# w_in in three loads, shifted V in halves, and a moved order table: an attention and gated feed-forward kernel on one core

## The chip, the cores and the metric

One core of one Trainium2 chip. The metric is the device time of one execution in microseconds (us), median over several runs. Lower is better. Each run is marked fast or slow: slow when it is more than 1.5% above the fastest run of the same kernel. Ratios are of fast runs; a median given below takes in every run. In the profile of before PE runs the matmuls (2,720), DVE, ACT and POOL the elementwise work (467, 474 and 203 operations), and SP issues all but a few transfers.

## The reference

Eight batches of 576 positions, eight heads of 64. Attention inside a window of 32 positions to either side, then a feed-forward block: a product with w_in (512 x 1024), a rectifier, a convolution over three positions in each feature, a sigmoid gate, a product with w_out (1024 x 512).

```python
mask = np.abs(pos[:, None] - pos[None, :]) <= 32
attn = softmax(np.where(mask, scale * q @ k.T, -1e9))
x = (attn @ v)                       # to (8, 576, 512)
h = np.maximum(x @ w_in, 0.0)
conv_out[:, s] = sum(conv_w[k] * hp[:, s + k] for k in range(3))   # hp: h with a zero row at each end
out = (h / (1.0 + np.exp(-conv_out))) @ w_out
```

## The kernel before

The program is a list of some 1,550 operations. A string, the order table, says in which order they are issued, on which engine (P is PE, V is DVE, S is ACT, G is POOL, D is a transfer on SP's queue, Q one on ACT's), and which buffers they take. Each engine works through its part strictly in that order.

```python
BUFS = {'st': 3, 'qkb': 5, 'qkT': 3, 'attn': 2, 'rec': 4, 'xn': 3, 'hT0': 8, 'hT1': 6, 'hT2': 6, 'cp': 2, 'gT': 4, 'y': 7}
ORDER = """
15D 11D0 12D 1F 17D 2F 13D1 2F 14D 7F 28G 0V 1P0 ...      # number, engine, buffers; "7F": seven filler matmuls
"""
    for number, engine, buffers in re.findall(r"(\d+)([A-Z])(\d*)", order):
        ...
        o.emit(engine)
```

V is needed in two alignments: `ve` as cast, and `vo` shifted by 64 positions across the partitions, which in batches 2 to 7 is a transfer:

```python
    def shift_v(b, c0, c1):
        op(f"vo hi {b} {c0} {c1}", lambda e: copy(e, vo[0:64, c0:c1], ve[64:128, c0:c1]), ...)
        op(f"vo lo {b} {c0} {c1}", lambda e: copy(e, vo[64:128, c0:c1], ve[0:64, c0 + 1:c1 + 1]), ...)
    ...
        for c in range(NBLK - 1) if b < 2 else (0,):
            shift_v(b, c, c + 1 if b < 2 else NBLK - 1)
```

The convolution of a unit (128 features of a chunk of 384 positions, 12 chunks of 8 units) can be done in six ways: each tap is a matmul with a diagonal matrix on PE, a multiplication on POOL, or a fused multiply and add on DVE.

```python
    #        PE taps      POOL taps  DVE taps
    TAPS = {
        "3": ((0, 1, 2), (), ()), "2": ((0, 2), (), (1,)), "1": ((0,), (), (1, 2)),
        "q": ((), (0, 2), (1,)), "r": ((), (0,), (1, 2)), "s": ((0,), (1, 2), ()),
    }
    CONV = ('33333333', '33q3323r23223321', ..., '2rrr2rrq')      # one letter for each unit
```

The softmax here doesn't subtract the row's maximum and nothing guards it: scores larger than these inputs give would overflow.

## Time and profile before

| | before |
|---|---|
| median of runs | 228.67 us |
| span of the profiled run | 225.6 us |
| PE, DVE, ACT, POOL busy | 211.5, 197.3, 187.5, 137.7 us |
| first input matmul, last matmul | 25.80, 221.71 us |

In a line of the timeline the columns are start, duration, engine, source line, operation, output and inputs, shapes, count and, in brackets, the idle time of the engine before it and what ended that. A line of the waits has the total, the number and the longest of a kind of wait. In the table by stage each engine has its busy us and its number of instructions. The prediction shows the lines of before.

One view that the prediction did not ask for is the table for the whole stretch from the first input matmul on:

```profile
26.00:226.00 200.00, 190.17 (x2391) 108.25 (x2389) 179.62 (x412) 168.79 (x429) 117.85 (x139) 1.00 0.80 202
```

From 25.80 us to PE's last matmul at 221.71 are 195.9 us, and PE is shown busy for 190.4 of them (190.17 in this view, and 0.2 before 26 us). That leaves 5.5 us in which it does nothing, a number that matters below.

### The profile page before, as it was taken

The page shows a single profiled execution, that of the slowest core. Times are in us where ns is not written, and L with a number is a line of the kernel's source. Part 1 is how long each engine was busy: PE and PEld are TensorE (multiplying, and loading weights), DVE is VectorE, ACT ScalarE, POOL GpSimd, SP SyncE. Part 2 cuts the span into 40 slices and gives each one's busy share as a digit, 9 for nine tenths or more (in the row PEclk, how much of TensorE's full clock was granted, in tenths as well). Part 3 has the DMA queues.
Part 4 walks back from the last instruction along what each step waited for, and adds up shares of the span by engine and source line. Part 5 has one row for each costly group of instructions (what it writes and reads, how often), then busy time and mean ns, then how long its engine had stood idle before and what let it go on. Part 6 is the DMA issues. An engine that isn't in the chain of part 4 may idle for free.

```text
span 225.6 us, 7189 instructions
## 1 busy us (share of the span) xinstructions
PE 211.5 (94%) x2720; PEld 122.9 (54%) x2720; DVE 197.3 (87%) x467; ACT 187.5 (83%) x474; POOL 137.7 (61%) x203
## 2 busy tenths in 40 slices
PE   7698899989989999989999998999999999999993
PEld 5366567658555655545555454545655565455541
DVE  6279869899999979797999788989999999899990
ACT  2689899998989889879889989689989999777642
POOL 5978654654376937695368736756386735566640
PEclk9889999999999999999999999999999999999999
DMA  6999999999989999999997989994535212501224
GB/s 201 331 285 358 355 266 281 321 308 253 290 170 324 317 175 287 236 306 224 288 347 129 202 278 358 182 231 147 144 36 118 99 46 49 175 1 49 93 101 178
DMA packets 66391, 48.16 MB, mean 214 GB/s; under 512 B 50781, under 2 KB 50805, under 8 KB 66357
## 3 DMA queue, kind: packets, MB, share of 16 engines
q1 hardware_dynamic: 64992, 46.32, 78.6%
q10 hardware_dynamic: 1364, 1.39, 2.9%
q8 instruction: 21, 0.34, 0.8%
q14 instruction: 14, 0.11, 0.2%
HBM read 32.52 MB, written 9.44 MB: 186 GB/s over the span
## 4 chain that ended last, share of the span: by engine, by line
PE 41%; DVE 18%; ACT 17%; DMA 13%; issue 5%; SPq 3%; POOL 2%; DVEq 0%; ACTq 0%; POOLq 0%
PE pf L232 41%; DMA st<-in_k_dram 7%; ACT attn L232 6%; DVE pf L232 5%; DVE gT L232 4%; SPq L232 3%; DMA out_dram<-y 3%; ACT xn L232 3%; DVE qkT L232 2%; ACT pf L232 2%; DMA vo<-ve 2%; DVE attn L232 2%; DVE xn L232 2%; ACT qkb L232 2%; ACT y L232 1%
## 5 line engine op out<-in xcount | busy, mean ns | idle before, releaser
L232 PE MATMUL pf<-xT,w_in_sb 128*128 128x385 bf16 (+2 forms) x416 | 73.4, 315 | 3.6 <-ACT hT L232 0.9
L232 PE MATMUL pf<-w_out_sb,gT 128*128 128x512 bf16 x288 | 72.2, 380 | 0.0
L232 POOL TENSOR_SCALAR cp<-hT,conv_w_sb 128x384 f32<-128x384 bf16 (+1 forms) x63 | 38.9, 622 | 46.1 <-ACT hT L232 20.2
L232 ACT ACTIVATE pf<-pf 128x384 f32<-128x384 f32 (+1 forms) x104 | 48.2, 477 | 13.1 <-DVE pf L232 11.1
L232 DVE SCALAR_TENSOR_TENSOR gT<-pf,hT 128x384 bf16<-128x384 f32 (+1 forms) x104 | 52.1, 517 | 5.5 <-ACT pf L232 5.1
L232 PEld LDWEIGHTS <-w_in_sb 128*128 128x128 bf16 x416 | 38.6, 98 | 27.8 <-issue 4.5
L232 ACT ACTIVATE attn<-pf 128x512 bf16<-128x512 f32 (+1 forms) x96 | 41.4, 522 | 1.8 <-PE pf L232 1.8
L232 ACT ACTIVATE hT<-pf 128x385 bf16<-128x385 f32 (+2 forms) x76 | 35.4, 487 | 6.0 <-PE pf L232 5.6
L232 PEld LDWEIGHTS <-gT 128*128 128x128 bf16 x288 | 26.0, 98 | 25.7 <-DVE gT L232 0.5
L232 DVE SCALAR_TENSOR_TENSOR pf<-hT,conv_w_sb,pf 128x384 f32<-128x384 bf16 (+1 forms) x61 | 34.7, 586 | 1.2 <-PE pf L232 1.1
L232 PE MATMUL pf<-hT,diag_w 128*128 128x384 bf16 (+1 forms) x153 | 30.9, 309 | 0.9 <-DVE xn L232 0.6
L232 POOL TENSOR_SCALAR qkb<-st 128x1152 bf16<-128x1152 f32 (+1 forms) x23 | 25.7, 1122 | 7.6 <-DMA st<-in_k_dram 3.2
L232 DVE COPY qkT<-pf 128x576 bf16<-128x576 bf16 x35 | 25.6, 750 | 4.9 <-PE pf L232 4.9
L232 POOL TENSOR_TENSOR cp<-cp,cp 128x384 f32<-128x384 f32 (+1 forms) x24 | 24.4, 1016 | 1.6
L232 DVE TENSOR_TENSOR attn<-attn,mask 128x1152 bf16<-128x1152 bf16 x26 | 23.0, 886 | 2.4 <-ACT attn L232 2.3
L232 ACT ACTIVATE xn<-pf,rec 128x64 bf16<-128x64 f32 x96 | 22.0, 360 | 1.5 <-DVE rec L232 1.5
L232 ACT COPY y<-pf 128x512 f32<-128x512 f32 x30 | 18.1, 605 | 3.9 <-PE pf L232 3.7
L232 DVE SCALAR_TENSOR_TENSOR pf<-hT,conv_w_sb,cp 128x384 f32<-128x384 bf16 (+1 forms) x35 | 21.2, 618 | 0.0
L232 POOL TENSOR_TENSOR attn<-attn,mask 128x1152 bf16<-128x1152 bf16 x6 | 14.2, 2371 | 8.4 <-ACT attn L232 8.4
L232 DVE TENSOR_TENSOR xn<-pf,rec 128x256 bf16<-128x256 f32 x48 | 18.9, 410 | 0.0
L232 ACT COPY qkT<-pf 128x576 bf16<-128x576 bf16 x29 | 18.6, 664 | 0.4 <-PE pf L232 0.2
L232 PEld LDWEIGHTS <-diag_w 128*128 128x128 bf16 x153 | 13.3, 97 | 9.8 <-issue 1.3
(49 smaller groups left out, 235.2 us busy)
## 6 DMA issues: line engine op xcount, KB each, us to landing
st<-in_q_dram SPq DMA_DIRECT2D x16, 576.0 KB, 6.8
out_dram<-y SPq DMA_DIRECT2D x36, 256.0 KB, 3.8
st<-in_k_dram SPq DMA_DIRECT2D x14, 576.0 KB, 8.2
vst<-in_v_dram SPq DMA_DIRECT2D x24, 256.0 KB, 7.0
vst<-in_v_dram SPq DMA_DIRECT2D x15, 192.0 KB, 5.7
vo<-ve SPq DMA_DIRECT2D x11, 260.0 KB, 5.6
st<-in_moe_w_in_dram SPq DMA_DIRECT2D x2, 1024.0 KB, 9.3
st<-in_moe_w_out_dram SPq DMA_DIRECT2D x2, 1024.0 KB, 9.4
```

Source lines behind the costliest of these rows:

```text
L232: return lambda *args, **kwargs: fixed(do(*args, **kwargs))
```

## The change

The intent: start the w_in casts after half a megabyte, let attention start on the first half of the shifted V, and shift convolution work from DVE to PE, with an order table made anew for it. The core of the diff (the order table itself is replaced nearly everywhere and cut here):

```diff
-BUFS = {'st': 3, 'qkb': 5, 'qkT': 3, 'attn': 2, 'rec': 4, 'xn': 3, 'hT0': 8, 'hT1': 6, 'hT2': 6, 'cp': 2, 'gT': 4, 'y': 7}
-TURNS = ('eeeee', 'eeede', 'eeeed', 'dedde', 'ddddd', 'ddddd', 'ddddd', 'edddd')
+BUFS = {'st': 3, 'qkb': 6, 'qkT': 4, 'attn': 2, 'rec': 9, 'xn': 2, 'hT0': 7, 'hT1': 8, 'hT2': 9, 'cp': 3, 'gT': 3, 'y': 5}
+TURNS = ('eeeee', 'eeede', 'eeeed', 'dddde', 'ddddd', 'ddddd', 'ddddd', 'deddd')
 CONV = (
     '33333333',
-    '33q3323r23223321',
-    's222r32q',
-    '1232s332',
-    '22q22q22',
+    '33q3323r23q23321',
+    's222r32s',
+    '12323332',
+    '22q22s22',
     'q31s2qrq',
-    '33212q2s',
-    'r2rq312q',
-    'qq23q1q2',
-    'r3rqrq23',
-    '12qrrq1q',
-    '2rrr2rrq',
+    '33222q2s',
+    '13rq312s',
+    'qq33q1q3',
+    'r2rqqq23',
+    '233rrs2q',
+    '3s112qrr',
 )
 ...
+    gpsimd.memset(outside, 0.0)           # and four affine_selects on it: for another form
+    ...                                   # of the mask, which no unit uses here
 ...
+    W_PARTS = {"in": ((0, 2), (2, 4), (4, MB)), "out": ((0, MB // 2), (MB // 2, MB))}
 ...
-        for c in range(NBLK - 1) if b < 2 else (0,):
-            shift_v(b, c, c + 1 if b < 2 else NBLK - 1)
+        for c in range(0, NBLK - 1, 1 if b < 2 else 2):
+            shift_v(b, c, c + (1 if b < 2 else 2))
```

## The prediction

> **What bounds the kernel now.** I read the page's busy shares and slices first, then the table by stage, then the start and the end of the timeline, and the waits last.
>
> ```profile
> PE 211.5 (94%) x2720; PEld 122.9 (54%) x2720; DVE 197.3 (87%) x467; ACT 187.5 (83%) x474; POOL 137.7 (61%) x203
> ...
> PEclk9889999999999999999999999999999999999999
> DMA  6999999999989999999997989994535212501224
> ```
>
> PE leads with 94%, but the matmul ends are modelled and 75 filler matmuls are in it, so it must be checked against DVE's 87%. The DMA engines are nearly full until slice 26 (about 146 us) and then empty out. The table by stage (window and its length, busy us of PE, PE's weight loads, DVE, ACT and POOL with instruction counts, then PE clock, DMA share, GB/s):
>
> ```profile
> 0.00:26.00 26.00, 21.33 (x331) 14.66 (x332) 17.63 (x57) 18.73 (x46) 19.87 (x65) 0.93 0.98 299
> 26.00:40.00 14.00, 13.87 (x191) 9.26 (x190) 10.97 (x22) 12.84 (x31) 7.31 (x11) 1.00 1.15 290
> 40.00:80.00 40.00, 38.48 (x618) 24.40 (x616) 39.28 (x103) 36.19 (x99) 24.72 (x28) 1.00 1.06 282
> 80.00:140.00 60.00, 56.60 (x794) 31.61 (x792) 52.01 (x124) 54.07 (x138) 38.22 (x41) 1.00 1.08 258
> 140.00:200.00 60.00, 59.50 (x685) 32.49 (x684) 57.98 (x128) 51.90 (x133) 36.66 (x46) 1.00 0.52 120
> 200.00:220.00 20.00, 20.00 (x103) 9.90 (x102) 19.38 (x38) 12.14 (x27) 10.94 (x15) 1.00 0.19 69
> ```
>
> From 40 us on, PE and DVE are both close to full, in turn: DVE is the fuller one at 40 to 80 us, PE elsewhere. Only the first 26 us have room, and there PE runs fillers. The start and end of PE's timeline:
>
> ```profile
> 25.80 2.13 PE L232 MATMUL pf<-xT,w_in_sb 128*128 128x385 bf16 x12 [0.29 <-DVE xT L232]
> ...
> 29.99 0.70 PE L232 MATMUL pf<-ident,qkb 64*128 64x64 bf16 x36
> 30.62 0.83 PE L232 MATMUL pf<-xT,w_in_sb 128*128 128x385 bf16 x4
> ```
> ```profile
> 209.94 1.48 PE L232 MATMUL pf<-xT,w_in_sb 128*128 128x385 bf16 x8
> ...
> 214.28 7.43 PE L232 MATMUL pf<-w_out_sb,gT 128*128 128x512 bf16 x33
> ```
>
> The first feed-forward matmul starts at 25.80 us and waits for xT, not for w_in. Back-to-back rates follow: 33 output matmuls in 7.43 us less one 0.38 latency, 0.220 us each; eight 385-column ones in 1.48 less 0.33, 0.165 each; 36 transposes in 0.63 (to the next start), 0.0175 each; scores, 18 in 0.39 elsewhere in the trace, 0.022; attention times V, pairs 0.031 apart, 0.016 each. With the counts of the groups, PE needs 288x0.220 = 63.4, input matmuls 352x0.165 + 64x0.083 = 63.4, diagonal (convolution) matmuls 118x0.165 + 35x0.083 = 22.4, attention and turns about 35: 184 us without fillers. An eighth of the attention (4.4) lies before 25.8, so PE has 179.8 us to do in the 195.7 us from 25.8 to its last matmul at about 221.5: 92%. DVE has 197.3 - 17.6 = 179.6 there: also 92%. ACT has 168.8. So from 25.8 us on the kernel is bound by PE and DVE together, with about 16 us of slack in pieces; startup is 25.8 us and the end about 4 us.
>
> The waits (total us, times, longest):
>
> ```profile
> DVE rec L232 <- PE pf L232: 2.7, 5, 1.7
> ...
> PE pf L232 <- DMA xT<-xn: 0.5, 1, 0.5
> ...
> POOL w_in_sb L232 <- DMA st<-in_moe_w_in_dram: 0.5, 1, 0.5
> ...
> PE pf L232 <- DMA vo<-ve: 0.3, 1, 0.3
> ```
>
> The two transfers that the change divides cost 0.3 us (shifted V, plus up to 2 us in the reciprocals behind it) and 0.5 us (w_in, on POOL).
>
> [...]
>
> **The change part by part.** I decoded the order table by the program's own numbering and counted operations per engine.
>
> *w_in in three loads.* Two transfers of 1 MB become 512 KB, 512 KB and 1 MB; same bytes. POOL's first cast starts at 18.53 when the first MB has landed. At about 340 GB/s (rate of slices 4 and 5) half a MB less is 1.5 us sooner. POOL also has other work there, and the first input matmul waits for xT. On the path: 0 to 0.5 us.
>
> *Shifted V in halves.* Before, 11 transfers of 260 KB (5.6 us median to landing); after, 23 of 130 KB and a small one. Bytes are the same to 0.1 MB of 48. Twelve more issues at 0.54 us put 6.5 us on SP's queue, which has long waits to hide them. The first half may land 0.5 us sooner, the second no sooner. Worth 0 to 0.7 us in all.
>
> *Startup order.* On ACT two more evictions of q/k transposes (about 0.54 each) and one xT eviction (0.65); DVE loses two evictions (1.5), one V shift (0.3) and two xT copies (1.0). DVE is the path from 19.4 to 25.8, ACT before. DVE's last mask of batch 0 began at 20.81 because DVE was occupied, not because ACT was late, so about 1 us of DVE is gained and part is handed to ACT. Fillers fall from 75 to 50, 17 of these ahead of the first transpose[...]. Sum: -0.5 us, give or take 1.5.
>
> *Kinds of convolution units.* Diagonal matmuls: full width 118 to 138, half width 35 to 33: +20x0.165 - 2x0.083 = +3.1 us of PE; one turn goes from PE to DMA, -0.2. Of these, the last two chunks take 8 to 19, +1.8 us in the stage with PE at 20.00 of 20.00.
> DVE: taps 96 to 81 at 0.61 = -9.2; sums 4 to 8 at 0.56 = +2.2; relus +2 at 0.55; normalisations +2 at 0.41; masks +1 at 0.89; q/k evictions -3 at 0.75; xT -2; V casts +2 at 0.45; one y copy +0.7: together -6.4 us, of which some 2.6 in the startup.
> ACT: +3 evictions, +1 cast, -2 normalisations of four pieces (0.92 each), -2 relus and small ones: +0.4. POOL: about -5, and it has slack.
>
> So after the startup PE's need rises from 179.8 to 182.7 and DVE's falls from 179.6 to 175.8.
>
> *Buffers.* Fewer y (7 to 5), gT (4 to 3), xn (3 to 2); more qkT, qkb, hT1, hT2, cp, rec. Stores land in 3.8 us and outputs are 36 in 180 us, so five y suffice on average; a copy can still wait where stores queue behind SP's other work.
>
> **The sum.** Added PE work +2.9; startup -0.5; both transfers -0.7; PE and DVE no longer equally full. That last term is a choice: of the 16 us of slack I expect about 4.5 to go, because DVE, which PE and ACT wait for, is at 90% instead of 92% and the order was moved throughout with it. Sum: 2.9 - 0.5 - 0.7 - 4.5 = -2.8, so 228.7 becomes about 225.8.
>
> **The rivals.** (1) PE is the whole bound: the added 2.9 us appears in full and slack stays at 16. For it: PE 20.00 of 20.00 in the end stage and 59.50 of 60 before it. Then 230 to 231. (2) DVE was the real bound, PE only filled its latencies: the 3.8 us less on DVE after the startup and the startup gain appear, with less waiting besides. For it: 39.28 of 40 at 40 to 80 us, 57.98 of 60 later, and the diagonal matmuls being bought on purpose. Then 221 to 224. (3) Loading is the bound until 146 us: DMA shares over 1.0, and the bytes do not change. Against it: PE's direct waits for DMA are under 1 us. Then the time stays at 228 whatever the order. (4) Fewer buffers make new waits (ACT or DVE for y or gT behind a store): +1 to +3.
>
> **Range and chances.** Two percent under 228.67 is 224.1; that needs 4.6 us, rival 2 or a startup shorter by over 2 us. Two percent over is 233.2, which needs rivals 1 and 4 together. Range 221.5 to 229.5. Chances: faster 0.28, within 0.68, slower 0.04.
>
> **What would show it.** First input matmul at 25 to 26 us; diagonal matmuls 138 of full width; DVE about 191 us, PE's busy less by its fillers (some 4 us) and more by 3; PE's waits for vo gone; the last 33 or so output matmuls still back to back. Wrong if the first input matmul moves by over 2 us, if 40 to 140 us changes its PE fill by more than 4 us, or if waits for y or gT appear.

Cut from the text: under the startup order, the clause for a term of +0.3 us, a lower clock on the first transposes, which was the author's estimate and not shown by a trace. That term is still inside the startup's -0.5 us, and so inside the sum, which came to -2.8 us: 228.7 to about 225.8.

## The result, and the profile after

The changed kernel is correct and slower: 240.55 us (238.49 to 242.12, four runs, one of them slow) against 228.77 us. The ratio is 1.0494, 95% interval 1.0413 to 1.0575. A ratio here is the mean time of one kernel's fast runs over the mean of the other's of the same rounds, so it is not quite the ratio of the medians. The profiled run is a fast one.

The page of the changed kernel, busy shares and slices:

```profile
PE 215.2 (90%) x2709; PEld 122.7 (51%) x2709; DVE 197.0 (82%) x460; ACT 187.7 (78%) x468; POOL 135.5 (57%) x206
...
PEclk9999799999999999999999979999999999999999
```

PE's share fell from 94 to 90%, although it has more to do. The clock row has two dips, in slices 5 and 24. The table by stage:

```profile
40.00:80.00 40.00, 36.92 (x538) 23.38 (x535) 35.72 (x90) 35.52 (x98) 23.41 (x28) 1.00 0.96 263
80.00:140.00 60.00, 54.38 (x804) 30.54 (x805) 52.07 (x119) 51.69 (x124) 34.32 (x36) 1.00 0.96 232
...
28.00:240.00 212.00, 197.82 (x2407) 111.19 (x2405) 181.32 (x407) 167.48 (x420) 113.82 (x133) 0.98 0.73 192
```

Against before, PE's fill falls from 38.48 to 36.92 at 40 to 80 us and from 56.60 to 54.38 at 80 to 140. ACT falls with it, DVE falls at 40 to 80 us and stands at 52 at 80 to 140: no engine has become fuller there. DVE's busy time over the whole run is 197.0 us against 197.3, although it has 7 operations fewer; the prediction had about 191. The start of PE's timeline:

```profile
27.27 0.66 PE L234 MATMUL pf<-ident,qkb 64*128 64x64 bf16 x18 [1.17 <-POOL qkb L234]
...
28.06 3.96 PE L234 MATMUL pf<-xT,w_in_sb 128*128 128x385 bf16 x16
```

The first input matmul is at 28.06, not 25.80, and sixteen of them take 3.96 us where twelve took 2.13: this is half clock, shown as 0.50 from 27.05 to 30.46 us. PE waited 1.17 us for a cast on POOL just before it, and ACT's copy of the first block of xT, which stands ahead of it too, began at 26.71 us in place of 24.54. At the end 43 output matmuls run back to back from 225.83 us for 9.44 us, as the last 33 did before, so PE's last matmul ends at 235.27 us, 13.6 later. The account of these 13.6 us:

| term | before | after | difference |
|---|---|---|---|
| first input matmul | 25.80 | 28.06 | +2.3 |
| PE busy from there on | 190.4 | 197.8 | +7.4 |
| PE idle from there to its last matmul | 5.5 | 9.4 | +3.9 |

Of the +7.4 us busy, two spells of half clock (from 27.05 and from 139.69 us, each 3.41 us long at 0.50 in the trace, each thus worth 1.7 us of work) are 3.4, the added diagonal matmuls 2.9 by the prediction's count, and 1.1 I can't assign. The waits say where PE starved:

```profile
DVE rec L234 <- PE pf L234: 9.3, 8, 5.1
...
PE pf L234 <- DMA vo<-ve: 2.9, 2, 1.8
```

The waits for `vo`, which the prediction said would be gone, are now 2.9 us in place of 0.3. They lie in batch 5, as does DVE's longest wait of 5.1 us. Here is PE, then SP's queue:

```profile
139.72 0.26 PE L234 MATMUL pf<-vo,attn 128*64 128x65 bf16 x1 [1.79 <-DMA vo<-ve]
```
```profile
131.26 0.50 SPq L234 DMA_DIRECT2D vo<-ve  x1
131.85 1.25 SPq L234 DMA_TRANSPOSE xT<-xn  x1
133.15 0.58 SPq L234 DMA_DIRECT2D vst<-in_v_dram  x1
133.78 1.87 SPq L234 DMA_DIRECT2D vo<-ve  x3
```

The four halves of batch 5 are issued between 131.26 and 135.65 us, with a transposing transfer and a load between them, though the casts they copy from were done at 118 us. In SP's single queue they stand behind transposing transfers (the four issued from 128.03 to 137.05 us hold it for 1.25 to 1.35 us each) and behind loads of V.

A last view is my own: each PE operation that both traces have, matched by name, and by how much it starts later than before (median over the stretch, in us, by the time in the kernel before). I call it the ladder. An operation that was moved back in the order counts as late too, so a single column is exact only where the order is the same.

| kernel | 10-20 | 20-30 | 30-40 | 60-70 | 80-90 | 120-130 | 130-140 | 160-170 | 220-end |
|---|---|---|---|---|---|---|---|---|---|
| changed | +0.4 | +1.8 | +4.5 | +6.1 | +7.6 | +7.6 | +11.7 | +12.0 | +13.1 |

The loss comes in steps, and little of it is given back.

### The profile page after: what moved, and what is told of

Its sections match the earlier page's. It is cut to its first block, busy times and chain, and to the rows that moved or that the text cites. A ratio compares the mean times of both kernels' runs of the same rounds, so it can differ in the third digit from the quotient of the medians.

```text
span 239.3 us, 7142 instructions
## 1 busy us (share of the span) xinstructions
PE 215.2 (90%) x2709; PEld 122.7 (51%) x2709; DVE 197.0 (82%) x460; ACT 187.7 (78%) x468; POOL 135.5 (57%) x206
## 3 DMA queue, kind: packets, MB, share of 16 engines
HBM read 32.52 MB, written 9.44 MB: 175 GB/s over the span
## 4 chain that ended last, share of the span: by engine, by line
PE 55%; DMA 16%; DVE 11%; ACT 7%; SPq 6%; issue 3%; POOL 0%; ACTq 0%; DVEq 0%
PE pf L234 55%; DMA st<-in_q_dram 10%; SPq L234 6%; DMA st<-in_k_dram 4%; DVE gT L234 3%; DVE pf L234 2%; ACT pf L234 2%; DVE qkT L234 2%; DMA vo<-ve 2%; ACT qkb L234 1%; ACT attn L234 1%; DVE attn L234 1%; DVE hT L234 1%; ACT xn L234 1%; DVE vo L234 1%
## 5 line engine op out<-in xcount | busy, mean ns | idle before, releaser
L234 PE MATMUL pf<-xT,w_in_sb 128*128 128x385 bf16 (+2 forms) x416 | 75.7, 321 | 1.4 <-ACT attn L234 0.6
L234 ACT ACTIVATE pf<-pf 128x384 f32<-128x384 f32 (+1 forms) x104 | 46.6, 468 | 13.2 <-DVE pf L234 8.3
L234 PE MATMUL pf<-hT,diag_w 128*128 128x384 bf16 (+1 forms) x171 | 36.0, 313 | 3.3 <-ACT hT L234 1.9
L234 DVE SCALAR_TENSOR_TENSOR pf<-hT,conv_w_sb,pf 128x384 f32<-128x384 bf16 (+1 forms) x54 | 31.4, 588 | 1.1 <-PE pf L234 0.6
L234 DVE COPY qkT<-pf 128x576 bf16<-128x576 bf16 x32 | 23.5, 748 | 5.9 <-PE pf L234 5.8
L234 ACT COPY qkT<-pf 128x576 bf16<-128x576 bf16 x32 | 20.5, 653 | 4.4 <-PE pf L234 4.3
L234 DVE TENSOR_TENSOR attn<-attn,mask 128x1152 bf16<-128x1152 bf16 x27 | 21.1, 783 | 2.8 <-ACT attn L234 2.8
L234 PEld LDWEIGHTS <-diag_w 128*128 128x128 bf16 x171 | 15.4, 97 | 14.6 <-issue 3.7
L234 DVE SCALAR_TENSOR_TENSOR pf<-hT,conv_w_sb,cp 128x384 f32<-128x384 bf16 (+1 forms) x27 | 18.8, 707 | 0.7 <-issue 0.3
L234 PEld LDWEIGHTS <-attn 128*64 128x64 bf16 x576 | 12.4, 112 | 13.5 <-issue 8.9
```

What stands on the lines that cost most here:

```text
L234: return lambda *args, **kwargs: fixed(do(*args, **kwargs))
```

## The experiments

Eighteen kernels ran. "Changed" is the changed kernel, "before" the kernel before. Times are medians of four runs if nothing else is said. Runs of one group shared a chip (the last two runs of the fourth had one of their own), and ratios are to runs of before on that chip (median 227.5 to 228.8 us in every group; one execution of before in the second group took 403.48 us, counts as slow and is in no ratio). A half-clock spell comes in some runs of a kernel and not in others (the four runs of a_vo5 have mean clocks of 1.000, 0.989, 0.990 and 0.991), so a difference of less than about 2 us between two medians is not read as an effect; the ladders of profiled runs, where one sees which spells there were, are used for that.

### First group: what starts the lateness

The changed order puts a small shifted-V transfer of batch 0 on SP's queue ahead of the w_in loads. It might hold them up. Three runs place that one shift elsewhere. A fourth moves batch 5's halves.

**a_shift_dve**: changed, that shift back on DVE.

```diff
-37D
+37V
```

> The changed kernel with one V shift (batch 0, block 2, upper half) moved from SP's DMA queue back to DVE; nothing else. Queue theory: on SP's in-order queue this shift waited for the cast on ACT until 12.32 us and held back the w_in loads (12.90 instead of 8.70) and the batch 1 loads; undone, w_in is issued near 8.7, the first input matmul starts at about 26 us instead of 28.06 with the clock at full, and the time falls by 3 to 5 us, to 236 to 237. Rival (later work absorbs a late start because PE has slack later): the start moves but the time falls by less than 1.5 us. Rival (the new order is bound elsewhere in the startup): the first input matmul stays within 0.5 us of 28.

Measured: 242.81 us, ratio 1.0637 (1.0573 to 1.0700). Two to three us worse than changed. DVE now waits for a cast on ACT, in order:

```profile
11.91 1.09 DVE L232 COPY vo<-ve 64x520 bf16<-64x520 bf16 x1 [2.38 <-ACT ve L232]
```

Against changed, the ladder is +2.8 us at 10 to 20 us, then about +2.1 (between 1.8 and 3.6), and +2.1 at the end. A delay of 2 us made at 12 us is 2 us at the end: nothing later took it up.

**a_shift_actq**: changed, that shift issued from ACT's queue behind its cast (`37D` becomes `37Q`).

```diff
-37D
+37Q
```

> The changed kernel with the same V shift still a DMA but issued from ACT's queue, right behind the cast it waits for. Queue theory: it is the wait at the head of SP's queue that costs, not the transfer; so the gain is as large as with the shift on DVE, within 1 us (ACT pays about 0.4 us for the issue). Rival (the transfer itself delays the loads or the first attention-times-V): the first input matmul stays near 28 us and the time near 240.

Measured: 239.31 us, ratio 1.0484 (1.0398 to 1.0569), not to be told from changed. The w_in load was issued at 8.33 us, and the first input matmul came at 26.98; the mean clock of that run is 0.986. In this pair of profiles what stands ahead of w_in on the queue is about 1 us of the loss.

**b_shift_sp**: before, with that shift on SP ahead of w_in, as in changed.

```diff
-... 2F 37V 18D 55S ...
+... 2F 18D 37D 55S ...
```

> The kernel before with that one V shift moved from DVE to SP's queue, in front of the first w_in load, where the changed kernel has it. Queue theory: w_in is issued about 4 us later, the first input matmul 2 to 3 us later and at half clock, the time rises by 3 to 5 us to 232 to 234. Rival (slack absorbs it): less than 1.5 us.

Measured: 226.63 us, ratio 0.9951 (0.9877 to 1.0025). The load of w_in was issued at 11.74 us, 3 us later than in before, and still the first input matmul came sooner than before's 25.80:

```profile
25.42 2.13 PE L230 MATMUL pf<-xT,w_in_sb 128*128 128x385 bf16 x12 [0.37 <-DVE xT L230]
```

So the queue ahead of w_in is not what makes the start late.

**a_vo5**: changed, the four halves of batch 5's shift moved to right behind a load of V, ahead of the stores and transposing transfers.

```diff
-... 1875D ... 1876D ... 1878D ... 1877D ...
+... 2528D 1875D 1876D 1878D 1877D ...       # 2528: load v 6 2
```

> The changed kernel with the four half shifts of V of batch 5 moved forward on SP's queue, right behind the first V load of batch 6 (their casts are done at 118.2 us, but they were issued at 131.3 to 135.0 behind transposing DMAs). Queue theory: the stall at 137.8 to 139.7 us, 5.06 us of DVE idle and a half-clock spell go away, and the time falls by 3 to 4.5 us. Rival (that stall only moves work later that PE and DVE had slack for): under 1.5 us.

Measured: 237.41 us, ratio 1.0424 (1.0346 to 1.0501). The halves are issued 13 us sooner, and the wait for them is gone:

```profile
118.08 4.68 SPq L232 DMA_DIRECT2D vo<-ve  x4
```
```profile
135.38 0.82 PE L232 MATMUL pf<-xT,w_in_sb 128*128 128x385 bf16 x4 [1.45 <-ACT attn L232]
```

A wait for the attention of the batch (1.45 us) now shows at the place. This run's profile had no half-clock spell before its end (mean clock 1.000). Against changed, its ladder is -1.9 us from 30 to 80 us (the instructions are the same there; 0.7 of it is an earlier first input matmul, the rest the missing spell), shrinks to -1.0 by 130 us, and is -4.6 from 140 us on. The stall of batch 5, its spell included, was thus worth 3.6 us where it stood in this pair, and 2.7 if the early lead is taken off the end. In the ratios it is 0.7%, and their intervals overlap.

### Second group: one part of the change on the kernel before

**b_win3**: before with w_in in three loads (`W_PARTS` of the diff; the second load right behind the first).

```diff
-            for i in range(2):
-                load_w("in", i)
+            for i in range(3):                # parts (0, 2), (2, 4), (4, 8) of the 8 column blocks
+                load_w("in", i)
```

> The kernel before with w_in loaded in three transfers (512 KB, 512 KB, 1 MB; the second right behind the first on SP's queue) and nothing else. Theory A (the parts of the change are harmless, the new order costs): same time within 0.7%, POOL's first w_in cast 1 to 2 us earlier, first input matmul still at 25.4 to 26. Rival (the smaller transfers hold back the batch 1 loads behind them): first input matmul or the batch 1 transposes 1 us or more later, time up by 1 us or more.

Measured: 228.69 us, ratio 1.0059 (0.9995 to 1.0124). POOL's first w_in cast began at 18.73 us against 18.53, so the smaller load brought nothing: the cast waits its turn on POOL, behind two copies of V that run from 17.27 to 18.65 us. No gain, and no loss that this many runs can show.

**b_halves**: before with the shifts of batches 2 to 7 in halves, each pair at the place of the whole one.

```diff
-        for c in range(NBLK - 1) if b < 2 else (0,):
-            shift_v(b, c, c + 1 if b < 2 else NBLK - 1)
+        for c in range(0, NBLK - 1, 1 if b < 2 else 2):
+            shift_v(b, c, c + (1 if b < 2 else 2))
```

> The kernel before with every whole-batch shift of V (batches 2 to 7) in two halves, one right behind the other where the whole one was; nothing else. Theory A: within 0.7% of before; twelve more issues of 0.5 us are hidden in waits of SP's queue. Rival (SP's queue is full around 118 to 140 us, so twelve issues push the loads and turns behind them): up by 1 to 4 us, with a stall at attention times V of a middle batch.

Measured: 231.32 us, fast-run ratio 1.0089 (1.0005 to 1.0173), two of four runs slow (232.90, 234.93), the profiled one among them. Its ladder is level to 80 us and rises at 90 and at 140 us, each time with a half-clock spell after a wait (clock 0.50 for 3.41 us from 92.39 and from 140.18 us); the one at 90 us is a wait of PE for `vo` of 3.03 us. That run being slow, I only take from it that halves gain nothing even without the other changes; that they cost something by themselves is not ruled out.

**b_pe21**: before with 21 more matmuls of 385 columns, spread over the chunks as the change spreads its diagonal ones (results overwritten, so still correct).

```diff
+            if m < EXTRA.get(c, 0):      # {2: 1, 3: 2, 4: 1, 6: 1, 7: 3, 8: 2, 10: 7, 11: 4}
+                tensor.matmul(ps.ap[:, 0:n], w_in_sb[:, 0, m * 128:(m + 1) * 128], x_[:, 0, lo:hi], start=True, stop=True)
```

> The kernel before with 21 more 385-column matmuls on PE, in the chunks that the change gives more diagonal matmuls (one to seven input units of chunks 2, 3, 4, 6, 7, 8, 10, 11 compute their first term twice; the result is unchanged). PE-bound theory: each costs its 0.165 us, so the time rises by 3.0 to 3.6 us. Rival (PE has slack to hide them, as the 16 us of slack in the prediction said): by less than 1.5 us.

Measured: 228.78 us, ratio 1.0052 (0.9974 to 1.0130). 21 x 0.165 = 3.5 us of work cost about 1 us of time, by an interval that reaches from -0.6 to 3.0. The ladder shows how: -1.0 us at the start (its first input matmul came at 24.77 us, ahead of any added matmul), -2.5 us at 120 us, then up by 2.8 to +0.3 at the end. And all four runs had a mean clock of 0.999 or 1.000, where runs of before have mostly 0.99; why is open, so the early start is no gain of the added work. Four of the added matmuls (0.7 us) stand before 130 us, in chunks 2 to 4, and show no price. The other 17 (2.8 us) cost their whole price.

**b_pe21_dve11**: the same, with 11 taps of DVE left out in those chunks (a wrong result).

```diff
+                if (c, m, kk) in DROP:        # (3,0,2) (6,3,2) (7,0,2) (8,5,2) (8,2,1) (10,0,2) (10,3,2) ...
+                    return
```

> As the run before, and 11 tap operations of 0.61 us left out on DVE in the same chunks (a wrong result on purpose): what the new kinds of convolution units do to both engines, at the places of the old order. If DVE's relief pays for PE's added work, the time is within 1 us of before or below it; if PE alone binds, it stays 2.5 us or more above before. The prediction counted on some 4.5 us of lost slack from this and the new order; then it would be 1 us or more below before.

Measured: 230.42 us, ratio 1.0117 (1.0053 to 1.0181). Freeing 11 x 0.61 = 6.7 us of DVE gained nothing. Two spells of half clock (0.50, 3.41 us each) were in the profiled run, at 8.16 and 83.25 us, so the stage in question has to be read alone: against b_pe21 the ladder is +0.4 to +0.7 us from 10 to 80 us, jumps to +3.8 at 80 to 90 (PE waits 1.99 us for ACT, ACT 3.2 us for a load of k, and the second spell follows), and is +4.4 at 130 to 140 and +4.4 at the end. Ten of the 11 taps left out stand after 130 us, and there they bought nothing. This is the trade on which the prediction's main gain rested.

### Third group: the start, and a cut by stages

**a_warm**: changed with ten filler matmuls ahead of the first transposes of batch 1.

```diff
-161P...
+10F6 161P...        # 161: the transposes; 6: a free bank
```

> The changed kernel with ten more filler matmuls (into a free bank) just ahead of the first transposes of batch 1, so that PE has no idle stretch there. If the half clock at 27.05 to 30.46 us comes from that idle stretch and every microsecond lost by PE is carried to the end, the profile shows full clock at 27 us, the 16 first input matmuls take about 2.7 us in place of 3.96, and the whole is 1.3 to 1.9 us faster (about 238.8). Rival: the slack of the later stages takes such a delay up; then the first stage is shorter and the time stays within 0.5 us of 240.5.

Measured: 238.99 us, ratio 1.0481 (1.0408 to 1.0555). The start is as expected:

```profile
25.95 1.25 PE L232 MATMUL pf<-zero 128*128 128x256 bf16 x10
...
27.63 2.78 PE L232 MATMUL pf<-xT,w_in_sb 128*128 128x385 bf16 x16
```

Sixteen input matmuls take 2.78 us, not 3.96. The ladder against changed is -1.6 us at 30 to 60 us and -1.1 from 60 to 130. At 137.65 us this run had a spell of 6.83 us at clock 0.50, twice that of changed, and gave the gain back there. The medians differ by 1.6 us, but the intervals of the ratios overlap nearly wholly, so the worth at the end is not shown.

**a_nodead**: changed without the unused constant, 1.55 us on POOL at the start.

```diff
-    gpsimd.memset(outside, 0.0)
-    for half in range(2): ...            # four affine_selects
```

> The changed kernel without the new constant (one memset and four selects on POOL, 1.55 us, that nothing reads in this form of the masks). POOL's first cast of V then begins at about 3.8 us in place of 4.64, and its q/k casts and diagonals about 1 us sooner. If that accounts for the +0.8 us that PE is late at 15 to 25 us, and lateness is carried, the whole is 0.6 to 1.2 us faster. Rival: the start waits for loads and for ACT, so POOL's delay is hidden; then no op after 20 us moves by more than 0.3 us and the time stays within 0.3 us, beyond the luck of half-clock spells.

Measured: 241.79 us, ratio 1.0623 (1.0540 to 1.0706). Operations before 10 us are 0.7 us sooner, those from 10 us on are not. The constant is hidden. The profiled run had two spells of 6.83 us at clock 0.50 (from 26.44 and from 139.08 us), so its lateness is no sign of harm.

**a_headn**: the order of before up to the first input matmul, that of changed after it (constant left out). Buffers fitted without one reassignment.

```diff
-<changed: order and engines of the first 166 entries, to ph 0 0>
+<before: order and engines of the first 181 entries, to ph 0 0>
```

> Before's order and engines (and without the unused constant) up to the first input matmul, the changed order from there on; loads of w_in still in three. If the start is late by its order and the lateness is carried in full, the first input matmul starts at 25.4 to 26.5 us (28.06 in the changed kernel) and the whole is 3 to 4.5 us faster than the changed kernel (236 to 237.5). Rival: the later order is bound by itself (its 3 us more of PE work and its stalls), so a start that is earlier by 2 us only lengthens a wait later; then the lateness against the changed kernel shrinks to under 1 us by 130 us and the time is 239 or more.

Measured: 236.31 us, ratio 1.0355 (1.0270 to 1.0440; one of four runs slow). The first input matmul is at 26.58 us. The loads of w_in stay in three. The exchange of starts is worth 1.4% (1.0494 less 1.0355), about 3 us; the two intervals overlap a little.

**a_cut80n**: the order and kinds of before up to 80 us, those of changed after it.

```diff
-<changed: order, engines and kinds up to ph 3 0>
+<before: order, engines and kinds up to ph 3 0>
```

> Before's order, engines and kinds of units up to 80 us (its first input matmul of chunk 3), the changed order from there on, with the changed buffer counts throughout. If the loss is a sum of delays that are carried, this takes away what had gathered by 80 us (+7.6 us in the changed kernel's profile) and leaves the stall of batch 5 (some 3.5 to 5) and the added PE work in the back half (2.5): 233 to 235 us. Rival (the changed buffer counts, fewer xn, gT and y, make the loss): the time stays over 237, since the counts are the changed ones in both parts. Rival (the back half alone sets the time): also over 237.

Measured: 235.48 us, ratio 1.0348 (1.0268 to 1.0427), so half a us above what was expected. The profile had a wait of 2.05 us for a transposed x at 109.67 and a spell of half clock at 110.1 (0.50 for 3.41 us), which other kernels lack. The cut took less away than the +7.6 us that changed had at 80 us.

### Fourth group: the back half, and a try to beat both

**a_cut135n**: the same with the cut at 135 us.

```diff
-<changed: order, engines and kinds up to av 5 1 3>
+<before: order, engines and kinds up to av 5 1 3>
```

> Before's order and kinds up to 135 us, the changed order from there on (changed buffer counts, no unused constant). If PE is full in the back half and its added matmuls count there in full (some 15 matmuls of 385 columns, 2.5 us), this is 2 to 3.5 us slower than before: 230.5 to 232 us. Rival (my prediction's view: DVE's relief pays for PE's work in the back half): 228 us or less. Rival (fewer gT or y buffers make waits in the back half): over 233 us, with waits on y or gT in the profile.

Measured: 247.55 us, ratio 1.0815 (1.0729 to 1.0901). Later, not sooner, than the cut at 80: ACT's copies of outputs waited 12.6 us for stores, 7.6 in one go. The mixture has five y buffers, as changed has, under before's order, which had seven. So this run answers nothing about the back half; it was mended below.

**a_headn_vo5**: a_headn with the halves of batch 5 moved as in a_vo5.

```diff
+<a_headn, and behind load v 6 2:> 1875D 1876D 1878D 1877D
```

> Before's start, then the changed order with the shifted V halves of batch 5 moved right behind their loads. If the start (4 us) and the stall of batch 5 (3 us with its half-clock spell) are two losses that add up, 233 to 234.5 us. Rival: they are one loss seen twice (the stall only happens when the kernel runs late), so 236 to 237 as with the start alone.

Measured: 236.33 us, ratio 1.0337 (1.0258 to 1.0415; one run slow). Equal to a_headn. The two gains do not add: with the earlier start PE's waits for `vo` were already down from 2.9 to 1.1 us. The stall of batch 5 is in part what the late start turns into.

**b_ahead**: the mirror: the start of changed, then before's order, with changed's buffer counts.

```diff
-<before: order and engines up to ph 0 0>
+<changed: order and engines up to ph 0 0; BUFS of changed>
```

> The mirror of the exchange of starts: the changed order up to the first input matmul (with the unused constant), before's order and kinds after it, and the changed buffer counts throughout. If the start's lateness is carried in full, 2 to 4 us slower than before: 230.7 to 233 us, its ladder of lateness flat from 30 us to the end but for half-clock spells. Rival: the 16 us of slack that I predicted take it up: 228 to 229.5 us. If fewer xn, gT and y buffers harm before's order, over 234 us with waits on those.

Measured: 256.22 us, ratio 1.1246 (1.1161 to 1.1332). The y buffers again (21.9 us of waits, 10.7 in one). Up to 80 us, before any such wait, its ladder can be read: +0.7 us at 20 to 30 us, then between +0.6 and +1.0 to 80 us. Its first input matmul is at 26.52 us. The same start gave 28.06 in changed, 27.36 in a_vo5 and 27.63 in a_warm. The difference between these runs is in a load: that of q for batch 1, issued at 15.87 to 16.02 us in all four, landed at 23.85 here and at 24.43, 24.93 and 25.99 there. So part of the +2.3 us of changed is the luck of its profiled run. In eleven profiles with before's start the first input matmul came at 24.77 to 26.74 us (middle 25.8), in five with the changed start and its early shift at 26.52 to 28.06 (middle 27.6).

**c_pool4**: a try to beat both: b_shift_sp, with four units of chunks 8 to 11 (`2`) turned to kind `q`, taps from PE to POOL; five cp and, for want of memory, five y buffers.

```diff
-'cp': 2, 'y': 7      # units (8,7) (9,6) (10,1) (11,4): '2'
+'cp': 5, 'y': 5      # the four units: 'q', POOL steps behind the relu, tap, tanh and gate 12 entries later
```

> A try at a kernel that beats both: before, with the first shifted V on SP's queue (226.63 us in its own run) and four units of chunks 8 to 11 whose two PE taps go to POOL (PE -8 matmuls of 384 columns, 1.3 us; POOL +4x2.3 us; DVE the same number of taps), with five cp and five y buffers. If back-half PE work counts in full: 225 to 226.5 us. Rival: POOL's three steps in a row come too late for DVE's tap in those units, and DVE's queue waits for them: 228 or more.

Measured (six runs): 260.28 us, ratio 1.1410 (1.1349 to 1.1470). Two faults: five y buffers (17.5 us of waits for stores), and DVE waiting for POOL's three steps, 9.2 us in five waits. No verdict on the idea with enough memory.

**a_cut135yn**: a_cut135n with seven y buffers.

```diff
-'y': 5
+'y': 7
```

> Before's order and kinds up to 135 us, the changed order and its 2.5 us more PE work after it, and now seven y buffers. If PE's added work counts in full and nothing else is lost in the back half: 1.5 to 3.5 us slower than before (230 to 232 us) and the ladder of lateness rises by 2 to 3 us from 140 us to the end. Rival (DVE's relief pays for it): 228.5 us or less, ladder flat or falling.

Measured: 232.36 us, ratio 1.0225 (1.0158 to 1.0292; one run slow). That is 4.8 us over before's median, more than the 1.5 to 3.5 expected. No waits for stores, no spell before the end. Its table by stage from 26 us on:

```profile
26.00:135.00 109.00, 102.36 (x1507) 61.18 (x1506) 96.68 (x231) 96.42 (x246) 68.84 (x75) 1.00 1.08 263
135.00:200.00 65.00, 64.42 (x763) 35.22 (x761) 59.61 (x132) 55.19 (x142) 37.70 (x46) 1.00 0.57 137
200.00:220.00 20.00, 20.00 (x110) 10.57 (x108) 19.33 (x38) 11.67 (x27) 11.46 (x16) 1.00 0.17 62
220.00:240.00 20.00, 6.21 (x29) 2.65 (x27) 3.77 (x8) 3.52 (x7) 0.00 (x0) 0.93 0.21 79
```

PE's busy time sums to 102.36 + 64.42 + 20.00 + 6.21 = 193.0 us, 2.8 above before's 190.2 from 26 us on. From the letters of CONV, chunks 6 to 11 have 62 diagonal matmuls in changed and 46 before: 16 x 0.165 = 2.6 us. The ladder is +0.9 at 120 to 130, +2.4 at 130 to 140, +3.3 at 170 to 180 and +4.1 at the end. The rise of 3.2 us is about the added PE work and some waits around 133 us; this run has the changed order there too, so b_pe21 is the one that shows the price of the work alone.

**b_y5**: before with five y buffers in place of seven (two runs).

```diff
-'y': 7
+'y': 5          # the buffer digits of ten y copies reassigned, order untouched
```

> Before with five y buffers in place of seven and its order untouched. If the count is what spoilt the three runs: 8 to 20 us slower than before, with waits of ACT's y copies for stores near 90 and 180 us of 5 us and more. Rival (the counts are harmless, as I predicted): within 1 us of before.

Measured: 245.70 us, ratio 1.0835 (1.0781 to 1.0888): 18 us. In the waits:

```profile
ACT y L230 <- DMA out_dram<-y: 18.4, 4, 9.8
```

PE in turn waited 14.8 us for ACT's copies. The count explains most of what spoilt the three runs (b_ahead and c_pool4 lost 28 and 32 us, so not all). The changed kernel, under its own order, lives with five: its waits have none of ACT or DVE on a store. Before's table needs seven.

The ladders of the runs that tell the stages apart (in us against before):

| kernel | 20-30 | 30-40 | 60-70 | 80-90 | 120-130 | 130-140 | 160-170 | 220-end |
|---|---|---|---|---|---|---|---|---|
| changed | +1.8 | +4.5 | +6.1 | +7.6 | +7.6 | +11.7 | +12.0 | +13.1 |
| a_vo5 | +1.1 | +2.6 | +4.2 | +5.2 | +6.6 | +7.1 | +7.4 | +8.5 |
| a_headn | +0.8 | +1.9 | +3.6 | +4.1 | +5.6 | +6.4 | +7.0 | +8.1 |
| a_cut80n | +0.8 | +0.8 | +0.9 | +1.4 | +4.5 | +5.8 | +6.3 | +7.5 |
| a_cut135yn | -0.5 | 0.0 | +0.1 | +0.8 | +0.9 | +2.4 | +3.0 | +4.1 |

Where a kernel still follows before's order its row is level within 1 us, and it climbs under the changed order, a_cut80n only from 110 us on, at its wait and spell. By ratios to before: changed 1.0494, own start exchanged 1.0355, before's order to 80 us 1.0348, to 135 us 1.0225. The steps are 1.4, 0.1, 1.2 and, for what is left after 135 us, 2.25%. Each ratio is known to some 0.8%, so only the last is clear of noise by itself.

## Why the prediction was wrong, point by point

The prediction said 225.8 us, with 4% for slower by over 2%. The kernel is slower by 4.9%. Of its signs, the diagonal matmuls (138) and the output matmuls back to back at the end came true. The first input matmul (28.06 us, and a move of over 2 us was to mean that it is wrong), the waits for `vo` (2.9 us, not gone) and DVE's busy time (197.0 us, not 191) did not.

**The step that failed: "of the 16 us of slack I expect about 4.5 to go".** The slack grew. By the prediction's own measure, PE's need by back-to-back rates taken from the time between the first input matmul and the last matmul, it was 195.9 - 179.8 = 16.1 us before and is 207.2 - 182.7 = 24.5 us after: 8.4 more, not 4.5 less. In the profile these 8.4 are 3.9 of idle PE (5.5 to 9.4), 3.4 of half clock and 1.1 without a name. The profiled run was to end 2.8 us sooner and its last matmul came 13.6 later; of the 16.4 us between the two, this term is 12.9, the startup 2.8, and the gain of both transfers that did not come 0.7.

The ground that the prediction gave, DVE's relief, failed with it. Where the relief was real (b_pe21_dve11) it bought back nothing after 130 us. In the changed kernel it did not even come: the operations were counted rightly, but DVE's busy time from the first input matmul on went from 179.8 to 181.3 us where 175.8 was predicted. One part of that is visible: the 24 full-width taps that read a `cp` of POOL took 744 ns each on average; the 33 of before took 630 ns. The rest of the gap is open.

Nor were 16 us there to give way. After 130 us b_pe21 found none: 2.8 us of added work cost 2.8. The profile's idle time says the same: between 140 and 220 us PE is shown busy for all but 0.5 us of 80. Before 130 us the added work of b_pe21 was too small (0.7 us) to measure the slack.

**Startup, -0.5 give or take 1.5.** Measured +2.3 at the first input matmul in the profiled pair, +1.8 by the middles of several profiles: outside its own margin. The prediction took DVE for the path from 19.4 to 25.8 us and counted on the work handed to ACT as a gain. With two more evictions and the xT copies on it, ACT's copy of xT's first block, which the first input matmul needs, began at 25.64 to 26.74 us in the profiles with the changed start that leave the early shift alone, and at 23.99 to 25.83 with before's. In a_vo5 and b_ahead the first input matmul waits for that copy. In the changed profile the copy ends at 27.36, and the matmul comes 0.7 us later still, behind transposes that had waited for POOL's cast of the late q. Counting how much each engine gains and loses did not say which one the first matmul waits for afterwards.

**Half clock, 0.3 us.** The prediction saw it as a matter of the start alone; its 0.3 us was an estimate that no trace had shown. The trace of the changed kernel shows two spells of 3.41 us at 0.50, each following a wait of PE, one of 1.17 us and one of 1.79. They slow real matmuls (sixteen input matmuls in 3.96 us, against 2.78 at full clock in a_warm), so each is worth 1.7 us. The sum had one term of 0.3, and 3.4 was measured in that run (it is in the 12.9 above).

**Shifted V in halves, -0.7 to 0.** The bytes and issues were counted rightly: 23 transfers of 130 KB. What they do in SP's queue was not: four small transfers stood at 131 to 136 us behind transposing ones, and PE waited 2.9 us for `vo` in place of 0.3. Moving them (a_vo5) took 2.7 to 3.6 us off with the spell in the profiled pair; with the earlier start (a_headn_vo5) it took nothing off the median, so the late start and the queue share that loss.

**w_in in three, -0.5 to 0.** Nothing on the path, as was half expected: b_win3 shows no gain.

**Diagonal matmuls, +2.9 us on PE.** Right in size, and after 130 us such work is in the time in full: b_pe21 shows it alone (2.8 us of work, +2.8), and a_cut135yn agrees (+2.8 us busy, a ladder that rises by 3.2 from 120-130 us to the end). Rival 1, "PE is the whole bound", came closest in mechanism. Its 230 to 231 misses what no rival had: an order whose waits add up.

**DVE relief as the gain (rival 2).** Refuted for the stage after 130 us by b_pe21_dve11, where ten of its 11 taps lie: they bought nothing back of the added PE work. An engine that is full in step with another was not for that reason a second bound here. Rival 3 (the time stays whatever the order) falls too: the time did change, with DMA shares that fell from 1.06 and 1.08 to 0.96 at 40 to 140 us.

**Buffers harmless.** Right for the changed kernel, whose waits show none for a store. Wrong as a general reading: five y buffers under before's order cost 18 us (b_y5). "36 outputs in 180 us" is an average over a program whose stores queue behind loads: in b_y5 one was issued at 90.94 us, right behind loads of q and k at 89.81 and 90.44, and ACT's longest wait for a store was 9.76 us.

**Small slips that change nothing.** The listed terms of DVE add up to about -6.1, not -6.4 us; the new issues of `vo` are 13, not 12; and slices 4 and 5 show 355 to 358 GB/s, not 340.

What stays open: the rise of about 4 us between 35 and 130 us. It shows in a_headn (+1.9 to +5.6) with no spell (clock 1.00 up to 220 us) and no single large wait, only six waits of PE of 0.15 to 0.5 us for DVE and ACT between 46 and 62 us, 1.9 us in all, where before has two (0.75 us). The changed kernel and a_vo5 have the same six, so they belong to the order and not to one run. Which moved entries make them was not tried one by one. The 1.1 us of PE busy time without a name stays open too. No kernel here beats before by more than its spread; b_shift_sp, at 0.9951, may.

## What to carry to other kernels

Where every engine follows one fixed order, a delay of PE that nothing absorbs is still there at the end (a_shift_dve: 2.1 us for most of the run, and 2.1 at the end): find out how much idle time the bound engine really has before you count on it, stage by stage, and read it from the trace rather than from back-to-back rates (5.5 us against 16 here). Judge a moved entry by what stands behind it in its queue, and a small transfer by what stands ahead of it, not by its bytes (the 130 KB halves of batch 5 left PE waiting 2.9 us). Buffer counts and an order table that were tuned together belong together; take one from a different version and the other breaks (b_y5: 18 us).

## What the traces show of the clock, the busy time and the queue

- Half clock. No gap of PE in the 3.41 us just before the two spells of the changed kernel was longer than 1.17 us (26.10 to 27.27) and 1.79 us (to 139.72), but in all PE was busy for only 1.60 and 0.51 us of them. The two stretches, and the second spell (columns: window, length, then PE's busy us first; the clock is the third number from the end):

```profile
23.64:27.05 3.41, 1.60 (x21) 0.95 (x16) 2.51 (x7) 3.41 (x12) 1.61 (x2) 1.00 1.10 333
...
136.28:139.69 3.41, 0.51 (x10) 0.29 (x9) 0.00 (x0) 2.26 (x6) 2.18 (x3) 1.00 1.08 148
139.69:143.10 3.41, 3.38 (x30) 1.68 (x31) 1.78 (x8) 1.07 (x4) 0.00 (x0) 0.50 1.07 287
```

  In before, the spell from 9.70 to 13.11 us (0.50) follows 3.41 us with PE busy for 1.41. With ten fillers in the first place (a_warm, PE busy for 3.07 us from 25.01 to 28.42) the clock stayed at 1.00 there. A low share did not always bring a spell: in the changed kernel PE is busy for 1.16 us from 3.16 to 6.57 and for 1.72 from 6.57 to 9.98, and the clock stays at 1.00 to 27.05. What decides it is not shown.

- The spells differ from run to run, and a comparison must allow for that: the changed kernel's runs here had mean clocks from 0.972 to 0.993 and times from 242.12 to 238.49 us.
- Busy time. In this profile the 288 output matmuls are shown 380 ns long on average and start 220 ns apart, so busy time is not work. For slack it was still the closer measure: it left 5.5 us of idle time where back-to-back rates gave 16, and no slack was found after 130 us.
- A divided transfer needs a place in the issuing queue too: the four halves of batch 5 were issued 13 us after their casts (118.21 to 131.26 us), behind transposing transfers.
